# A hand-ordered attention and maxout kernel: another list of all work, three more query groups turned by DMA, six output tiles scaled on ScalarE

## The chip, the core and the metric

The program runs on one core of a Trainium2 chip. The core has a matrix engine (TensorE, PE in the profile), VectorE (DVE), ScalarE (ACT), GpSimd (POOL) and SyncE (SP), which here only issues DMA transfers. Matmuls write to PSUM, eight banks of 128 rows x 512 fp32; everything else lies in SBUF. The metric is the time of one execution on the device in microseconds, as the median of several runs.

## The reference

Four batches of 12544 queries, keys and values of 128 channels meet 49 agents per batch: the agents attend to the keys and values, the queries attend to the agents, and the result goes through a maxout layer of three 128 x 768 weights and an output weight.

```python
def sm(a, b):                      # softmax over the last axis
    s = scale * (a @ b.transpose(0, 2, 1))
    s = s - s.max(-1, keepdims=True)
    e = np.exp(s)
    return e / (e.sum(-1, keepdims=True) + 1e-09)
agent_v = sm(agents, k) @ v        # 49 x 128 for each batch
x = (sm(q, agents) @ agent_v).reshape(50176, 128)
h = np.maximum(np.maximum(x @ w1, x @ w2), x @ w3)
out = h @ w_out
```

All inputs and the output are float32; the kernel computes in bf16 with fp32 sums.

## The kernel before, in words

**Maxout by differences.** The kernel never forms `x`. For each batch it multiplies the normalised `agent_v` with three prepared matrices, w3-w1, w2-w1 and w1 @ w_out, into one tile `G` (49 agents, twice, in rows 0 to 48 and 64 to 112). With max(a, b, c) = a + max(0, c-a, b-a) a query's output is a linear part plus `wo` times max(relu(e G31), e G21), where `e` is the exponential of the query's 49 scores. The division by the sum of `e` comes last, when the output tile is scaled.

**Groups.** The 50176 queries are 49 groups of 8 tiles of 128 rows. For group `s` the steps are: load (`ql`), cast to bf16 on GpSimd (`qc`), turn so that channels are rows, scores (`sc`), exponential on ScalarE (`ex`), sums of `e` (`su`) and their reciprocals on VectorE (`re`). The turning is done in one of two ways: by eight TensorE transposes and a VectorE copy from PSUM (`qt`, `qe`), or, for the groups listed in `TURNED`, by one transposing DMA from the SP queue (`qd`).

**Six hidden blocks per group.** Block `f` has 128 hidden units for 1024 queries. In blocks other than 4, TensorE makes `u` (difference 31) into two banks, ScalarE takes relu of it to SBUF (`a`, tile `AS`), TensorE makes `v` (difference 21) into two other banks and VectorE takes the maximum of both (`x`, tile `R`). In block 4 ScalarE applies relu in place, TensorE adds `v` on top, and ScalarE applies relu again. So a group has five 128 x 1024 operations on VectorE and seven on ScalarE. `u` and `v` use rows 0 to 48 and 64 to 112 of TensorE as two 64-row halves that run beside each other.

**Output.** The output tile of a group is two banks, o = 0 and 1, each for every second tile of 128 queries. `li` adds the linear part and `p.s.o.f` the product of block `f` with `wo`. `ROWS` has a letter per group and block: with `f` a product is four matmuls with 128 rows, with `r` it is eight matmuls with 64 rows, in pairs that write to both banks at once. After the last product VectorE multiplies each bank with the reciprocals into SBUF (`ov.s.o`, tile `OS`, nine buffers) and SP stores the tile (`st`).

**Keys and values** of a batch come in chunks of up to 9 tiles of 128 rows: loads `kl`, `vl`, casts `kc`, `vc`, for batches 1 to 3 a transposing DMA of the keys (`kt`, tile `KT`), scores `ks`, exponential `kx`, product with the values `kv`, and sums `va`, `ea`. Batch 0 is done first, with TensorE transposes; the chunks of batch b+1 are mixed among the query groups of batch b.

**What sets the order.** `graph` lists every step with its engine and needs. `ORDER` is one written-out list of all 2876 steps; each engine takes its steps in that order, and the numbers behind a slash give the buffers or PSUM banks. `Plan.waits` derives the semaphore waits from the list. The `cost` and `serve` values belong to the planner that wrote the list; the program that is built doesn't use them. All instructions are issued through one recorder, so the profile gives them one line (L379 before), and groups are told apart by tile names: `ps` is PSUM, `EQ` the query exponentials, `LD` the load buffers, `QB`, `QT`, `KB`, `KT` the cast and turned tiles, `RC` the reciprocals.

Of the kernel before, what the change touches and what calls it, by code (L numbers as in the profile page):

```python
# [195 lines left out]
def dma(kb):  # L196
    return dict(cost=(0.45, 1.0), serve=kb / 415.0)


def graph(plan, em):  # L200
    add = plan.add
# [62 lines left out]
    for b in range(1, B):  # L264
        ch = chunks(b)
        for g, (t0, n) in enumerate(ch):
# [6 lines left out]
            add(f"kt{r}", SP, em.turn_by_dma("kb", "kT", r, n), (1.3, 1.0), after=[f"kc{r}"], new=[("KT", f"kT{r}")], use=[f"kb{r}"],  # L273
# [3 lines left out]
                use=[m])  # L277
# [25 lines left out]
    for s in range(NQ):  # L303
# [4 lines left out]
        if s in TURNED:  # L308
            add(f"qd.{s}", SP, em.turn_by_dma("qb.", "qT.", s, GT), (1.3, 1.0), after=[f"qc.{s}"], new=[("QT", f"qT.{s}")], use=[f"qb.{s}"],
                serve=0.255 * GT)  # L310
# [81 lines left out]
class Emit:  # L392
# [422 lines left out]
to0.3 vl0.8/2 kl0.0/8 kc0.8/0 ke0.9/2 kv0.10 kv0.5 kt0.8/0,1 ke0.2/1 vc0.3/0 kx0.11/0 kx0.7/2 vc0.2/3 ke0.8/0 wm.6/1 ks0.9/3 to0.7
kv0.3 ks0.2/7 to0.11 kt0.6/5,6 kl0.1/4 qt.0/4 ks0.8/0 kv0.11 qe.0/2 vl0.9/12 kc0.4/1 kx0.2/3 to0.2 kv0.2 kx0.8/1 kt0.4/0,1 wm.2/4
ke0.4/2 ke0.6/0 kc0.0/0 vc0.7/2 kx0.9/3 vc0.8/3 vl0.0/11 vc0.4/1 vl0.6/10 wm.1/0 ks0.4/0 ks0.6/1 sc.0/5 vl0.1/3 to0.8 kx0.6/0
ex.0/0 lw3a/7 lw1a/9 kv0.7 kt0.0/3,4 kc0.1/1 lw1b kv0.8 kt0.1/5,6 kx0.4/2 ke0.0/1 vc0.9/2 ks0.0/3 wm.0/1 to0.4 ke0.1/0 lw2a/1
kx0.0/1 lw3b kv0.4 to0.9 to0.0 ks0.1/3 vc0.0/3 kx0.1/2 vc0.6/1 vc0.1/0 lw2b wm.4/6 kv0.9 su.0/3 to0.6 to0.1 rs0/0 ql.1/6 qc.1/0
cw1 kv0.6 rc0 d31a kv0.0 kv0.1 nr0/0 d21a d31b gpa/1 lwo/5 tw1/6 re.0/0 d32 kl1.0/2 ql.2/4 cwo ew1 gpc/0 kc1.0/2 gva u.0.1/4,5  # L820
gpb/1 gvb d21b gvc u.0.2/6,7 v.0.1/2,3 a.0.1/1 kl1.1/11 u.0.0/4,5 gpd/0 x.0.1/12 qt.1/1 qe.1/2 a.0.2/0 qc.2/2 gvd u.0.3/6,7
a.0.0/2 a.0.3/1 v.0.0/2,3 pl/4 sc.1/5 x.0.0/8 vl1.0/0 el kc1.1/0 u.0.4/6,7 ex.1/1 a.0.4 kt1.0/0 v.0.3/0,1 u.0.5/4,5 x.0.3/0
v.0.2/2,3 v.0.4 u.1.1/0,1 x.0.2/5 a.0.5/2 qt.2/4 kt1.1/2 x.0.4/1 p.0.0.3/5 qe.2/2 v.0.5/2,3 a.1.1/0 u.1.0/6,7 x.0.5/6 vc1.0/3
vl1.1/2 ql.3/3 p.0.0.1 p.0.0.4 p.0.0.2 a.1.0/1 v.1.1/0,1 sc.2/4 x.1.1/4 gl/2 p.0.0.0 kl1.2/11 vl1.2/7 vc1.1/1 ks1.0/3 gvl
v.1.0/6,7 li.0/2 x.1.0/7 ex.2/2 u.1.3/0,1 kx1.0/2 su.1/4 kv1.0 re.1/3 va1.0/0 qc.3/0 p.0.0.5 p.0.1.2 kc1.2/2 u.1.2/6,7 ql.4/6
a.1.3/0 ov.0.0/0 v.1.3/3,4 u.1.4/0,1 a.1.2/1 a.1.4 x.1.3/5 p.0.1.5 ks1.1/5 p.0.1.1 p.0.1.3 v.1.2/6,7 ea1.0/0 u.1.5/3,4 kx1.1/0
p.0.1.4 p.0.1.0 kv1.1 v.1.4 vc1.2/3 x.1.2/6 v.1.5/6,7 a.1.5/0 u.2.1/3,4 x.1.4/11 kt1.2/0 a.2.1/1 ov.0.1 va1.1 p.1.0.0/2 qt.3/5
x.1.5/9 p.1.0.4 u.2.2/0,1 a.2.2/2 u.2.0/6,7 v.2.1/3,4 qe.3/0 p.1.0.2 qc.4/1 su.2/5 p.1.0.1 p.1.0.3 p.1.0.5 kl1.3/2 kl1.5/3 x.2.1/8
v.2.0/0,1 kl1.4/5 li.1/4 a.2.0/0 u.2.3/6,7 p.1.1.4 p.1.1.3 re.2/0 a.2.3/1 sc.3/5 x.2.0/0 v.2.2/0,1 u.2.4/6,7 ov.1.0/4 v.2.3/2,3
x.2.2/10 ex.3/1 kc1.3/2 p.1.1.2 p.1.1.0 ks1.2/5 u.2.5/0,1 a.2.4 kx1.2/3 v.2.4 a.2.5/2 p.1.1.5 p.1.1.1 kv1.2 x.2.3/6 ov.1.1 va1.2  # L830
x.2.4/12 v.2.5/2,3 kc1.4/1 u.3.1/0,1 qt.4/4 x.2.5/9 a.3.1/0 u.3.0/5,6 p.2.0.2/7 p.2.0.1 qe.4/0 su.3/3 v.3.1/0,1 a.3.0/2 vl1.3/11
re.3/1 sc.4/2 v.3.0/3,4 x.3.1/2 u.3.3/5,6 p.2.0.0 p.2.0.4 ex.4/0 p.2.0.5/0 li.2 v.3.3/1,2 a.3.3/1 x.3.0/1 u.3.2/5,6 a.3.2/0 ea1.1
p.2.0.3 u.3.4/3,4 p.2.1.3 p.2.1.5 a.3.4 x.3.3/7 ql.5/12 p.2.1.1 vl1.4/9 v.3.2/1,2 ov.2.0/8 u.3.5/5,6 qc.5/2 p.2.1.4 kt1.3/0
p.2.1.2 p.2.1.0 a.3.5/2 x.3.2/5 v.3.4 x.3.4/3 ov.2.1 v.3.5/1,2 u.4.1/6,7 ql.6/2 qt.5/5 p.3.0.0/0 x.3.5/4 a.4.1/1 ks1.3/3 ql.7/0
# [204 lines left out]
```

## Time and profile before

| | us |
|---|---|
| median of 3 runs (lowest, highest) | 446.41 (445.01, 449.0) |
| the profiled execution | 445.94 |
| its span | 444.1 |
| TensorE matmuls busy | 413.0 |
| TensorE weight loads busy | 258.4 |
| VectorE busy | 393.5 |
| ScalarE busy | 391.4 |
| GpSimd busy | 170.2 |

The span runs from the first to the last instruction of the profiled execution; the 1.8 us around it are launch and end. Busy times of one engine are the union of its instructions, so overlapping ones count once, and matmul ends are modelled. A group's row gives its count, its busy time, the mean of one instruction and the idle time just before it with what ended that. In the table by stretches each engine's busy us in the stretch are followed by the number of instructions in brackets, then come the granted TensorE clock, the mean busy share of the DMA engines and GB/s. The chain of work that ended last puts 65% of the span on TensorE, 10% on DMA, 9% on VectorE, 5% each on ScalarE and GpSimd.

### The profile page before, as it was taken

The numbers are of one execution on the slowest core, as the hardware profiler recorded it, in microseconds if no ns is written. First come the engines' busy times: TensorE is split into PE (matmuls) and PEld (weight loads), VectorE is DVE, ScalarE is ACT, GpSimd is POOL, SyncE is SP. The second block draws the span as 40 slices with busy tenths as digits, with TensorE's granted clock in tenths as the row PEclk, the third lists the DMA queues.
The fourth block names the chain that finished last, engine by engine and source line by source line (L and its number), as shares of the span: only waits on it lengthen the run. The fifth ranks groups of instructions, "written<-read, shape, count | busy, mean of one in ns | idle before, by whom it ended". The sixth has DMA issues, their size and how long they took to land.

```text
span 444.1 us, 14119 instructions
## 1 busy us (share of the span) xinstructions
PE 413.0 (93%) x6128; PEld 258.4 (58%) x6128; DVE 393.5 (89%) x502; ACT 391.4 (88%) x464; POOL 170.2 (38%) x177
## 2 busy tenths in 40 slices
PE   0687999999999989999899999999999999999994
PEld 0564556666666656656566666656655555655574
DVE  2336999999999989999899999999999999999994
ACT  1269999899989889999799899999999999999992
POOL 4531557645665525461844534256221000200000
PEclk9889999999999999999999999999999999999999
DMA  8999999999999999999999999999979445556333
GB/s 308 408 412 386 266 335 291 323 348 315 341 285 359 391 259 268 373 269 355 297 304 403 268 294 315 303 249 246 278 163 301 158 73 161 127 84 180 143 130 111
DMA packets 91768, 120.75 MB, mean 272 GB/s; under 512 B 65143, under 2 KB 67899, under 8 KB 91707
## 3 DMA queue, kind: packets, MB, share of 16 engines
q1 hardware_dynamic: 91504, 119.75, 91.3%
q8 instruction: 48, 0.79, 0.7%
q10 hardware_dynamic: 203, 0.10, 0.1%
q14 instruction: 13, 0.11, 0.1%
HBM read 78.74 MB, written 25.69 MB: 235 GB/s over the span
## 4 chain that ended last, share of the span: by engine, by line
PE 65%; DMA 10%; DVE 9%; ACT 5%; POOL 5%; issue 4%; SPq 1%; POOLq 0%; DVEq 0%; ACTq 0%
PE ps L379 65%; DVE R L379 6%; ACT AS L379 4%; DMA LD<-in_q_dram 3%; DMA out_dram<-OS 2%; DVE OS L379 2%; DMA KT<-KB 2%; DMA LD<-in_v_dram 2%; DMA LD<-in_k_dram 1%; POOL QB L379 1%; POOL VB L379 1%; SPq L379 1%; POOL EA L379 1%; POOL KB L379 1%; ACT R L379 1%
## 5 line engine op out<-in xcount | busy, mean ns | idle before, releaser
L379 DVE TENSOR_TENSOR R<-ps,AS 128x1024 bf16<-128x1024 f32 x245 | 293.9, 1219 | 13.9 <-PE ps L379 9.4
L379 ACT ACTIVATE AS<-ps 128x1024 bf16<-128x1024 f32 x245 | 245.3, 1029 | 16.2 <-PE ps L379 12.4
L379 PE MATMUL ps<-EQ,G 49*128 49x512 bf16 (+1 forms) x1248 | 196.6, 370 | 3.6 <-DVE OS L379 0.5
L379 PE MATMUL ps<-wo_bf,R 128*128 128x128 bf16 (+1 forms) x2984 | 187.4, 218 | 1.0 <-issue 0.8
L379 PEld LDWEIGHTS ps<-wo_bf,R 128*128 128x128 bf16 (+1 forms) x2984 | 137.1, 96 | 57.2 <-issue 37.3
L379 PEld LDWEIGHTS ps<-EQ,G 49*128 49x128 bf16 x1248 | 55.5, 93 | 70.2 <-DVE R L379 21.3
L379 POOL CAST QB<-LD 128x1024 bf16<-128x1024 f32 x49 | 51.3, 1050 | 106.3 <-DMA LD<-in_q_dram 53.0
L379 POOL CAST KB<-LD 128x1152 bf16<-128x1152 f32 (+2 forms) x45 | 50.0, 1119 | 59.4 <-DMA LD<-in_k_dram 36.3
L379 DVE TENSOR_TENSOR OS<-ps,RC 128x512 f32<-128x512 f32 x98 | 66.5, 680 | 2.9 <-DMA out_dram<-OS 1.7
L379 ACT ACTIVATE R<-ps 128x1024 bf16<-128x1024 f32 x49 | 50.2, 1025 | 2.1 <-PE ps L379 1.8
L379 ACT ACTIVATE ps<-ps 128x1024 f32<-128x1024 f32 x49 | 50.0, 1020 | 1.8 <-PE ps L379 1.2
L379 POOL CAST VB<-LD 128x1152 bf16<-128x1152 f32 (+1 forms) x33 | 37.3, 1139 | 33.0 <-DMA LD<-in_v_dram 28.5
L379 POOL TENSOR_TENSOR EA<-EA,EK 128x441 f32<-128x441 f32 x27 | 27.7, 1024 | 13.6 <-ACT EK L379 13.2
L379 ACT ACTIVATE EQ<-ps 128x512 bf16<-128x512 f32 x49 | 29.5, 601 | 2.3 <-PE ps L379 1.9
L379 ACT ACTIVATE EK<-ps 128x441 bf16<-128x441 f32 (+2 forms) x45 | 23.8, 533 | 4.4 <-PE ps L379 4.2
L379 ACT ACTIVATE VB<-LD 128x1152 bf16<-128x1152 f32 (+1 forms) x12 | 12.3, 1051 | 17.1 <-DMA LD<-in_v_dram 14.0
L379 PE MATMUL ps<-agT,KT 128*128 128x49 bf16 x392 | 17.4, 185 | 5.7 <-DVE KT L379 3.3
L379 DVE COPY QT<-ps 128x1024 bf16<-128x1024 bf16 x27 | 18.4, 681 | 3.2 <-PE ps L379 3.1
L379 PE MATMUL ps<-QT,agT 128*64 128x512 bf16 (+1 forms) x104 | 19.9, 388 | 0.0
L379 PEld LDWEIGHTS ps<-agT,KT 128*128 128x128 bf16 x392 | 14.3, 97 | 9.0 <-DVE KT L379 4.0
L379 PE MATMUL ps<-G,EQ 49*128 49x128 bf16 x392 | 19.1, 217 | 0.0
L379 DVE COPY KT<-ps 128x1152 bf16<-128x1152 bf16 (+1 forms) x12 | 8.2, 699 | 12.0 <-PE ps L379 12.0
(58 smaller groups left out, 187.4 us busy)
## 6 DMA issues: line engine op xcount, KB each, us to landing
LD<-in_q_dram SPq DMA_DIRECT2D x48, 512.0 KB, 7.2
out_dram<-OS SPq DMA_DIRECT2D x48, 512.0 KB, 5.8
LD<-in_k_dram SPq DMA_DIRECT2D x40, 576.0 KB, 7.3
LD<-in_v_dram SPq DMA_DIRECT2D x40, 576.0 KB, 8.9
LD<-in_k_dram SPq DMA_DIRECT2D x3, 512.0 KB, 7.0
LD<-in_v_dram SPq DMA_DIRECT2D x3, 512.0 KB, 7.5
LD<-in_moe_w_dram SPq DMA_DIRECT2D x6, 192.0 KB, 13.5
KT<-KB SPq DMA_TRANSPOSE x33, 7.3
```

What stands on the lines that cost most here:

```text
L379: i = call(*args, **named)
```

## The change

1. Groups 24, 27 and 29 join `TURNED`: each loses eight TensorE transposes and one VectorE copy and gains one transposing DMA on the SP queue.
2. `ROWS` has 89 letters `r` where it had 79, in other places.
3. `SCALER` is new: of the 98 output banks, six are scaled by ScalarE instead of VectorE, bank 1 of groups 3, 14, 25, 32, 47 and 48. There it takes four activations of 128 x 128 with the reciprocal as a per-row scale from SBUF, where VectorE does one 128 x 512 multiplication.
4. `ORDER` is a new list of all steps, with other buffers.
5. The planner's latency of a DMA goes from 1.0 to 1.9 us; only the list shows it.

```diff
-TURNED = (22, 25, 28, *range(30, 49))
+TURNED = (22, 24, 25, 27, 28, 29, 30, 31, 32, 33, 34, 35, 36, 37, 38, 39, 40, 41, 42, 43, 44, 45, 46, 47, 48,)
 ROWS = """
-ffffff ffffff fffrfr ffffrf ffffff rfffrf ffffff rfffrr ffffrf ffffff ffffff ffffff rfrfrr ffffff frfffr ffffff ffffff rrffff
+ffffff frrrrf ffffrf fffrff ffffff fffrrr ffffff frffrf rfrfff rffrff ffffff ffffff rfrfrr ffffff fffffr ffffff ffffff frrfff
...
+SCALER = """
+dd dd dd ad dd dd dd dd dd dd dd dd dd dd ad dd dd dd dd dd dd dd dd dd dd ad dd dd dd dd dd dd ad dd dd dd dd dd dd dd dd dd dd
+dd dd dd dd da da
+""".split()
...
 def dma(kb):
-    return dict(cost=(0.45, 1.0), serve=kb / 415.0)
+    return dict(cost=(0.45, 1.9), serve=kb / 415.0)
...
         for o in range(2):
-            add(f"ov.{s}.{o}", DVE, em.out_scale(s, o), (0.605, 0.705), use=[both[o], f"rc.{s}", plan.tile("OS", f"os.{s}")],
+            eng = ACT if SCALER[s][o] == "a" else DVE
+            add(f"ov.{s}.{o}", eng, em.out_scale(s, o, eng), (0.66, 0.82) if eng == ACT else (0.605, 0.705), use=[both[o], f"rc.{s}", plan.tile("OS", f"os.{s}")],
...
-    def out_scale(self, s, o):
-        def fn():
-            self.nc.vector.tensor_tensor(out=self.t[f"os.{s}"][:, o::2, :], in0=self.t[f"o.{s}.{o}"].rearrange("p (j c) -> p j c", c=C),
-                                         in1=self.t[f"rc.{s}"][:, 4 * o:4 * o + 4].unsqueeze(2).to_broadcast([P, 4, C]), op=ALU.mult)
+    def out_scale(self, s, o, eng):
+        def fn():
+            src, out, rc = self.t[f"o.{s}.{o}"].rearrange("p (j c) -> p j c", c=C), self.t[f"os.{s}"], self.t[f"rc.{s}"]
+            if eng == ACT:
+                for j in range(4):
+                    self.nc.scalar.activation(out[:, 2 * j + o, :], src[:, j, :], AF.Copy, scale=rc[:, 4 * o + j:4 * o + j + 1])
+            else:
+                self.nc.vector.tensor_tensor(out=out[:, o::2, :], in0=src, in1=rc[:, 4 * o:4 * o + 4].unsqueeze(2).to_broadcast([P, 4, C]),
+                                             op=ALU.mult)
         return fn
...
 ORDER = """
-kl0.5/4 id0 id ql.0/1 agl kl0.3/8 kc0.5/0 kl0.11/12 kc0.3/1 kl0.2/2 agc kl0.10/0 ones kl0.6/3 agt/0 qc.0/0 vl0.3/9 vl0.11/8
```

What the new list moves is shown at three places. First VectorE where the products of batch 2 leave PSUM (`CAST G_146`) and group 22 and 23 are in work. Before:

```order
266 L379 TENSOR_TENSOR R_123<-ps,AS_115 128x1024
267 L379 CAST G_146<-ps 128x384 x2
268 L379 TENSOR_TENSOR R_127<-ps,AS_116 128x1024
269 L379 COPY QT_105<-ps 128x1024
270 L379 TENSOR_TENSOR R_124<-ps,AS_117 128x1024
271 L379 COPY VA_148<-ps 128x49
272 L379 TENSOR_TENSOR R_129<-ps,AS_116 128x1024
```

The same place now:

```order
262 L384 CAST G_146<-ps 128x384
263 L384 TENSOR_TENSOR R_119<-ps,AS_117 128x1024
264 L384 CAST G_146<-ps 128x384
265 L384 TENSOR_TENSOR R_120<-ps,AS_115 128x1024
266 L384 COPY VA_148<-ps 128x49
267 L384 TENSOR_TENSOR R_128<-ps,AS_117 128x1024
```

The copy of group 24's turned queries (`COPY QT_105`) is gone between two maxima; what stood around it stays. Next the SP queue around the store of group 14, which is row 143 before (`OS_138`) and row 128 now (`OS_140`). `LD` are loads, `out_dram` stores. Before:

```order
135 L379 DMA out_dram<-OS_136 128x1024
136 L379 DMA LD_89<-in_k_dram 128x1152
137 L379 DMA LD_86<-in_k_dram 128x1152
138 L379 DMA LD_84<-in_v_dram 128x1152
139 L379 DMA LD_79<-in_q_dram 128x1024
140 L379 DMA LD_83<-in_v_dram 128x1152
141 L379 DMA LD_90<-in_q_dram 128x1024
142 L379 DMA LD_78<-in_q_dram 128x1024
143 L379 DMA out_dram<-OS_138 128x1024
144 L379 DMA_TRANSPOSE KT_102<-KB_94 128x9x128
```

Now:

```order
124 L384 DMA_TRANSPOSE KT_101<-KB_96 128x9x128
125 L384 DMA LD_88<-in_k_dram 128x1152
126 L384 DMA LD_89<-in_v_dram 128x1152
127 L384 DMA LD_84<-in_k_dram 128x1152
128 L384 DMA out_dram<-OS_140 128x1024
129 L384 DMA_TRANSPOSE KT_103<-KB_95 128x9x128
130 L384 DMA out_dram<-OS_141 128x1024
131 L384 DMA LD_85<-in_k_dram 128x1024
132 L384 DMA_TRANSPOSE KT_102<-KB_94 128x9x128
```

Group 14's store stood behind seven loads in a row and now stands behind three. The buffer that it empties is next written by group 19's scaling before and by group 17's now; counted in entries of the list, the store lies 25 ahead of that before and 52 now. Last, ScalarE's end, from the relus of group 48's hidden blocks on (`ps<-ps` is the first relu of its block 4, `R` the second). Before:

```order
460 L379 ACTIVATE AS_117<-ps 128x1024
461 L379 ACTIVATE AS_116<-ps 128x1024
462 L379 ACTIVATE ps<-ps 128x1024
463 L379 ACTIVATE R_127<-ps 128x1024
464 L806 UNCONDITIONAL_BRANCH
```

Now:

```order
465 L384 ACTIVATE AS_117<-ps 128x1024
466 L384 ACTIVATE ps<-ps 128x1024
467 L384 ACTIVATE OS_143<-ps,RC_131 128x128 x4
468 L384 ACTIVATE R_128<-ps 128x1024
469 L384 ACTIVATE OS_135<-ps,RC_132 128x128 x4
470 L816 UNCONDITIONAL_BRANCH
```

Four activations of group 47's output tile now stand between the two relus of group 48's block 4, and four of group 48's own tile behind them.

More of the change, by code (lines that the diff above doesn't have):

```diff
@@ L272, in graph @@
             add(f"vc{r}", POOL, em.cast("v", "vb", b, t0, n, POOL, 0, n), c, after=[f"vl{r}"], new=[("VB", f"vb{r}")], use=[f"v{r}"])
-            add(f"kt{r}", SP, em.turn_by_dma("kb", "kT", r, n), (1.3, 1.0), after=[f"kc{r}"], new=[("KT", f"kT{r}")], use=[f"kb{r}"],
+            add(f"kt{r}", SP, em.turn_by_dma("kb", "kT", r, n), (1.3, 1.9), after=[f"kc{r}"], new=[("KT", f"kT{r}")], use=[f"kb{r}"],
                 serve=0.255 * n)
@@ L308, in graph @@
         if s in TURNED:
-            add(f"qd.{s}", SP, em.turn_by_dma("qb.", "qT.", s, GT), (1.3, 1.0), after=[f"qc.{s}"], new=[("QT", f"qT.{s}")], use=[f"qb.{s}"],
+            add(f"qd.{s}", SP, em.turn_by_dma("qb.", "qT.", s, GT), (1.3, 1.9), after=[f"qc.{s}"], new=[("QT", f"qT.{s}")], use=[f"qb.{s}"],
                 serve=0.255 * GT)
@@ L815 @@
[L815 to L822, printed above, removed]
@@ L1007 @@
-x.48.4/9 p.48.1.3 p.48.0.2 st.42 p.48.1.2 ov.47.0 p.48.1.5 p.48.1.4 p.48.0.3 p.48.0.5 p.48.0.4 st.47 ov.48.1/8 ov.48.0 st.48
+kl0.5/0 kl0.6/11 agl kl0.0/10 id0 kc0.5/1 kl0.10/1 ql.0/6 ones agc id kl0.11/0 agt/0 kc0.6/0 prep kc0.0/2 kl0.8/9 kl0.4/3 qc.0/2
+vl0.11/4 kt0.5/5,6 kt0.0/3,4 kt0.6/1,2 vl0.0/5 vc0.0/3 kc0.10/2 vl0.4/7 wm.3/0 kc0.8/1 qt.0/0 wm.0/7 wm.5/7 kc0.4/0 ke0.0/1
+ke0.6/2 ke0.5/0 qe.0/0 kl0.3/9 ks0.0/7 vc0.4/2 kt0.8/1,2 kt0.10/3,4 sc.0/0 vl0.10/1 ke0.10/1 vl0.3/11 kl0.1/6 ks0.10/3 vd0.11/1
```

385 lines of the change are left out of this document (196 added, 189 removed).

## The prediction

> **What bounds the kernel now.** I read the page's busy shares first, then the busy time in stretches of 40 us.
>
> ```profile
> PE 413.0 (93%) x6128; PEld 258.4 (58%) x6128; DVE 393.5 (89%) x502; ACT 391.4 (88%) x464; POOL 170.2 (38%) x177
> ...
> core 0: us, PE busy (x) PEld busy (x) DVE busy (x) ACT busy (x) POOL busy (x), PEclk, DMA share, GB/s
> 60.00:100.00 40.00, 39.96 (x587) 25.07 (x584) 38.64 (x48) 36.93 (x45) 23.94 (x23) 1.00 1.10 323
> 100.00:140.00 40.00, 39.89 (x583) 25.04 (x581) 38.01 (x52) 37.13 (x45) 22.54 (x25) 1.00 1.10 331
> 140.00:180.00 40.00, 38.62 (x574) 24.41 (x572) 37.42 (x49) 36.34 (x44) 20.44 (x21) 1.00 1.08 297
> 180.00:220.00 40.00, 38.55 (x546) 23.62 (x541) 36.72 (x47) 36.42 (x45) 20.54 (x20) 1.00 1.04 337
> 220.00:260.00 40.00, 39.87 (x623) 25.21 (x623) 38.90 (x49) 37.62 (x47) 18.14 (x21) 1.00 1.09 315
> 260.00:300.00 40.00, 39.49 (x569) 23.91 (x566) 37.93 (x48) 38.23 (x45) 17.55 (x17) 1.00 1.14 287
> 300.00:340.00 40.00, 39.44 (x571) 23.67 (x570) 37.88 (x49) 38.48 (x48) 14.89 (x18) 1.00 0.99 245
> ...
> sum 360.00, PE 354.97 PEld 217.72 DVE 343.10 ACT 338.89 POOL 145.34; mean PE 39.44 PEld 24.19 DVE 38.12 ACT 37.65 POOL 16.15
> ```
>
> From 60 to 420 us three engines are nearly full at once: in the sum row TensorE's matmuls cover 354.97 of 360, VectorE 343.10, ScalarE 338.89. No single engine can be relieved for its full worth. Two stretches stand out: from 140 to 220 us TensorE is idle 1.38 + 1.45 = 2.83 us, while the stretches around them (100:140, 220:260) lose 0.11 and 0.13. The table of waits and the chain say what happened there:
>
> ```profile
> PEld ps L379 <- DVE R L379: 22.8, 87, 0.5
> PEld ps L379 <- ACT AS L379: 16.0, 58, 0.8
> ...
> DVE OS L379 <- DMA out_dram<-OS: 1.7, 1, 1.7
> ...
> PE ps L379 <- DMA KT<-KB: 1.2, 1, 1.2
> ...
> 154.01 7.46 DMA KT<-KB
> ...
> 205.39 10.45 DMA out_dram<-OS
> ...
> 215.93 0.69 DVE OS L379
> ```
>
> TensorE stood 1.2 us for one transposed key tile, issued at 154.01, and VectorE 1.7 us for one store, issued at 205.39 and landed 10.45 us later. The waits of the full engines on one another are many and short: TensorE's 87 on VectorE's `R` sum to 22.8 us and none is over 0.5.
>
> **The change, part by part.** The sum is made against the profiled execution, 445.94 us (span 444.1). That is 0.47 below the median of 446.41 and inside its runs (445.01 to 449.0), so I don't shift it. The prices come from the groups by shape:
>
> ```profile
> L379 DVE TENSOR_TENSOR R<-ps,AS 128x1024 bf16<-128x1024 f32 x245 | 293.9, 1219 | 13.9 <-PE ps L379 9.4 <-ACT AS L379 0.3
> L379 PE MATMUL ps<-wo_bf,R 128*128 128x128 bf16 x1720 | 134.6, 220 | 0.0
> L379 PEld LDWEIGHTS ps<-wo_bf,R 128*128 128x128 bf16 x1720 | 97.5, 97 | 42.8 <-issue 35.2 <-DVE OS L379 4.4 <-DVE RC L379 0.7
> L379 DVE TENSOR_TENSOR OS<-ps,RC 128x512 f32<-128x512 f32 x98 | 66.5, 680 | 2.9 <-DMA out_dram<-OS 1.7 <-PE ps L379 0.6
> L379 PE MATMUL ps<-wo_bf,R 64*128 64x128 bf16 x1264 | 53.4, 216 | 1.0 <-issue 0.8 <-ACT EQ L379 0.2
> L379 DVE COPY QT<-ps 128x1024 bf16<-128x1024 bf16 x27 | 18.4, 681 | 3.2 <-PE ps L379 3.1
> L379 PE MATMUL ps<-ident,QB 128*128 128x128 bf16 x216 | 16.6, 219 | 0.5 <-POOL QB L379 0.5
> L379 ACT ACTIVATE G<-ps 128x128 bf16<-128x128 f32 x4 | 1.2, 295 | 0.2 <-PE ps L379 0.2
> ```
>
> *New places of transfers, -2.0 us.* The two DMA stalls above cost 2.83 - 0.24 = 2.6 us. In the new list the store of group 14 stands behind three loads, not seven, and the closest reuse of an output buffer after its store is 24 list entries away, not 8; the closest use of a transposed key tile is 19 away, not 8. So I count most of the 2.6 as gone. Bounds: -2.8, and +2.8 if as many new stalls appear elsewhere.
>
> *Groups 24, 27, 29 turned by DMA, -1.5 us.* VectorE loses 3 copies of 0.681 = 2.04 us; TensorE loses 3 x 8 transposes at 16.6 / 216 = 0.077, 1.85 us. Both run in stretches where both engines are over 94% busy, so nearly all of it is on the path. Three transposes join the SP queue; the loads queued behind them are covered as long as the DMA is ahead (second rival). Bounds 0 and -2.04.
>
> *Four output tiles in mid-run (groups 3, 14, 25, 32), 0.* VectorE saves 0.68 each. ScalarE gains four activations of 128x128; the nearest row, the `G` evacuation of that size, gives 4 x 0.295 = 1.18. Their scale operand comes from SBUF per row, which no activation of this trace has. Groups 3 and 14 end in 60:100 and 140:180, where ScalarE is idle 3.07 and 3.66 us and VectorE 1.36 and 2.58: a gain. Groups 25 and 32 end in 260:300 and 300:340, where ScalarE is idle 1.77 and 1.52 and VectorE 2.07 and 2.12: a loss. Queued behind each tile on ScalarE is the next relu, and behind that the matmul that needs its bank. Bounds 4 x -0.68 = -2.7 and 4 x 1.18 = +4.7. The Trainium skill (ScalarE: Activation LUTs, What ACT_TABLE_LOAD costs) prices an activation with immediate scale at 186 + 0.833 N ns, adds 93 ns for a per-row pointer operand and lets neighbours overlap by 93. For 128 columns without the pointer that is 293 ns, and the trace's 295 agrees; with it, an estimate from that page is 4 x 386 - 3 x 93 = 1265 ns a tile, 0.09 above my 1.18, by which the four would cost 0.3 us more. The same page's rules advise VectorE for multiplications, which speaks against this part of the change.
>
> *Two output tiles at the end (groups 47, 48), +0.5 us.* The last us of the timeline:
>
> ```profile
> 435.95 0.40 PE L379 MATMUL ps<-wo_bf,R 64*128 64x128 bf16 x8
> 436.15 1.23 DVE L379 TENSOR_TENSOR R<-ps,AS 128x1024 bf16<-128x1024 f32 x1 [0.94 <-PE ps L379]
> ...
> 436.61 1.02 ACT L379 ACTIVATE R<-ps 128x1024 bf16<-128x1024 f32 x1 [1.54 <-PE ps L379]
> 437.29 0.68 DVE L379 TENSOR_TENSOR OS<-ps,RC 128x512 f32<-128x512 f32 x1
> ...
> 438.12 1.36 DVE L379 TENSOR_TENSOR OS<-ps,RC 128x512 f32<-128x512 f32 x2 [0.15 <-PE ps L379]
> ```
>
> Now ScalarE waits for group 47's last matmuls (436.35), scales for 1.18 until 437.5 and only then does the last relu of group 48, which started at 436.61: 0.9 us late. Behind it stand the last matmuls and both scalings. These run side by side, but ScalarE's takes 1.18 where VectorE's two took 1.36, so 0.2 returns: +0.7. Since that matmul may come earlier in the new list, I take +0.5; bounds -0.7 (one VectorE tile) and +0.9.
>
> *Ten more blocks in 64-row form, 0.* A pair block takes 53.4 / 79 = 0.68 us of matmul, a full one 134.6 / 215 = 0.63. What a full block costs besides is the weight load's 35.2 us of issue wait. Counted over TensorE's list, though, the passes between 64-row and 128-row work were 380 and are 379. The Trainium skill (TensorEngine Tiling (Array Packing), Tiling Modes) says that changing the mode drains TensorE; that fits the issue wait, and by it only the passes count, which gives 0 here as well. Bounds: ten times 35.2 / 215 = 0.16 us, -1.6, and 10 x 0.05 = +0.5.
>
> *Start, 0.* Both lists load the first batch's 24 key and value chunks and the weights before the second batch, and the first hidden blocks keep their order. The DMA, not the list, sets this stretch. Bounds +-1.
>
> Sum: 445.94 - 2.0 - 1.5 + 0 + 0.5 = 442.9, say **443 us**.
>
> **The rivals.** *VectorE alone sets the pace.* Then nine operations less count in full, 3 x 0.681 + 6 x 0.68 = 6.1 us, and the stalls' 2.6: 445.94 - 8.7 = 437.2. For it: VectorE is fuller than ScalarE in most stretches, and TensorE's weight loads fill only 217.72 of 360 us. The Trainium skill (Perfetto Trace Analysis, Identifying the Most-Contended Engine) calls matmul busy time a bad measure and weight-load busy time a good one; by it TensorE, at 60%, isn't the bound and VectorE, at 95%, is. Against it: the waits of VectorE's longest group end with TensorE (9.4 of 13.9 us).
>
> *The DMA becomes the bound: slower.* Its rows:
>
> ```profile
> q1 hardware_dynamic: 91504, 119.75, 91.3%
> ...
> KT<-KB SPq DMA_TRANSPOSE x33, 7.3
> ...
> QT<-QB SPq DMA_TRANSPOSE x22, 4.7
> ...
> 10.00:40.00 30.00, 21.67 (x327) 16.83 (x328) 11.34 (x18) 17.34 (x26) 10.76 (x11) 0.89 1.03 406
> ```
>
> The transposes move about 15.4 MB by their tiles' shapes, so plain transfers are 119.75 - 15.4 = 104.4 MB. At the 406 GB/s of 10:40 they take 257 us, 265 with its share of 1.03; q1's share is 0.913 x 444.1 = 405 us, which leaves 140 / 55 = 2.55 us of all engines for a transpose. Three add 7.7 us to a stretch whose share is over 1 from 60 to 300. If loads can't run ahead enough there, the path gets it: 445.94 + 7.7 = 453.6. The point from which it decides is TensorE waiting for key or query tiles in every group. Against it: those waits are 1.2 us now, and the DMA share falls to 0.99 after 300, so stores can move there.
>
> *ScalarE's tiles cost in full*: the first two terms as forecast, then +4.7 and +0.9: 445.94 - 3.5 + 5.6 = 448.0. For it: ScalarE is only 4 us emptier than VectorE over 360. *The list gains nothing*: other stalls for the old ones, 446.
>
> **How the numbers follow.** Forecast 0.39, its own range 440 to 446; VectorE 0.20; DMA 0.14; ScalarE 0.10; no gain 0.17. One per cent of 446.41 is 4.46, about what a measurement here tells from no change: under 441.95 is faster, over 450.87 slower. Of the forecast 0.17 lies under 441.95; with VectorE's 0.20 faster is 0.37. Slower is DMA's 0.14 and 0.03 of ScalarE's, 0.17. The rest, 0.46, is within 1%. For 8 in 10 the range runs from 436 (leaves out about 0.06, VectorE's case with more) to 451 (leaves out DMA's 0.14).
>
> **What would show it.** In the new profile: TensorE over 39.7 of 40 us in the stretches between 140 and 220, and VectorE's wait for a store gone (first term); 24 query copies and 25 query transposes with TensorE's waits on them still near 1 us (second); 24 activations of 128x128 with ScalarE no fuller than VectorE (third); the end of the last scaling over 1.85 us after the last relu's end or not (fourth); the weight load's issue wait near 35 us (fifth). The prediction is wrong if the stretches between 60 and 300 lose more than 0.5 us each, which the list alone can do in a way that no row of before shows.

## The result, and the profile after

The changed kernel takes **444.24 us** (median of 16 runs, 443.07 to 446.67), the kernel before 447.65 us (16 runs, 445.01 to 451.67). The ratio is 0.9929 with a 95% interval from 0.9902 to 0.9956: 0.7% faster, which is within one per cent. The forecast was 443 us, range 436 to 451, with "within 1%" the likeliest of the three outcomes. Three executions of the kernel before in the later calls were in a slower state and are left out of its medians.

The two profiled executions differ less than the medians: 445.94 us before and 445.17 after (spans 444.1 and 443.3). The one of before lies in the lower half of its runs, the one of after in the upper. (The section on the change says bank 1 for all six tiles of ScalarE. It is bank 0 in groups 3, 14, 25 and 32, and bank 1 in groups 47 and 48; nothing hangs on it.)

Busy time of the changed kernel in stretches of 40 us (the columns are those of the same view in the prediction):

```profile
60.00:100.00 40.00, 39.64 (x615) 25.28 (x612) 37.74 (x48) 37.87 (x47) 20.23 (x20) 1.00 1.06 319
100.00:140.00 40.00, 39.81 (x607) 25.42 (x605) 38.57 (x51) 37.57 (x46) 25.35 (x27) 1.00 1.06 330
140.00:180.00 40.00, 39.26 (x565) 24.50 (x567) 38.12 (x50) 37.92 (x50) 20.77 (x21) 1.00 1.03 286
180.00:220.00 40.00, 39.91 (x562) 25.35 (x560) 38.72 (x50) 37.70 (x46) 18.27 (x18) 1.00 1.13 331
220.00:260.00 40.00, 39.14 (x628) 24.27 (x627) 37.98 (x48) 37.42 (x46) 20.42 (x23) 1.00 1.08 330
260.00:300.00 40.00, 39.33 (x577) 23.82 (x575) 36.70 (x46) 39.03 (x50) 18.79 (x18) 1.00 1.15 276
300.00:340.00 40.00, 39.66 (x562) 23.83 (x560) 37.33 (x47) 39.23 (x52) 12.62 (x15) 1.00 1.04 295
...
sum 360.00, PE 356.21 PEld 219.82 DVE 342.90 ACT 344.88 POOL 144.60; mean PE 39.58 PEld 24.42 DVE 38.10 ACT 38.32 POOL 16.07
```

TensorE's idle time from 140 to 220 us fell from 2.83 to 0.74 + 0.09 = 0.83 us. Over the 360 us ScalarE has 6 us more work (344.88 against 338.89) and VectorE the same as before (342.90).

The gain is small in the two profiles because it is gained in one place and lost in another. The next two fences are ScalarE's rows in the timeline where the hidden blocks of group 1 and of group 48 begin (the first relu of each), before and after:

```profile
49.50 1.97 ACT L379 ACTIVATE AS<-ps 128x1024 bf16<-128x1024 f32 x2
...
428.46 1.03 ACT L379 ACTIVATE AS<-ps 128x1024 bf16<-128x1024 f32 x1
```

```profile
52.70 1.02 ACT L384 ACTIVATE AS<-ps 128x1024 bf16<-128x1024 f32 x1 [0.29 <-PE ps L384]
...
428.42 1.03 ACT L384 ACTIVATE AS<-ps 128x1024 bf16<-128x1024 f32 x1
```

Group 1 begins 3.20 us later than before. From there to group 48 the changed kernel needs 375.72 us where the old one needed 378.96: 3.24 less. From group 48's first relu to the end of the span it is 443.3 - 428.42 = 14.88 against 15.64: 0.76 less. Together +3.20 - 3.24 - 0.76 = -0.80, which is the difference of the spans.

The loss at the start shows in the column of the granted clock (the third from the right). Before and after, from 35 us:

```profile
35.00:40.00 5.00, 3.63 (x75) 2.29 (x72) 2.25 (x4) 4.96 (x7) 0.00 (x0) 1.00 1.04 379
40.00:45.00 5.00, 3.94 (x41) 1.74 (x38) 4.17 (x11) 4.36 (x6) 2.22 (x2) 1.00 1.07 382
45.00:50.00 5.00, 4.42 (x40) 1.81 (x36) 4.98 (x6) 4.80 (x7) 3.82 (x4) 1.00 0.90 233
```

```profile
35.00:40.00 5.00, 1.95 (x36) 1.39 (x32) 1.14 (x4) 3.72 (x4) 0.00 (x0) 0.72 1.04 389
40.00:45.00 5.00, 4.70 (x36) 1.86 (x32) 3.74 (x10) 3.57 (x6) 1.29 (x2) 0.50 1.07 380
45.00:50.00 5.00, 5.00 (x30) 2.04 (x30) 3.38 (x5) 3.57 (x6) 3.91 (x4) 0.50 0.93 271
```

TensorE's row in the timeline of the changed kernel after its longest pause there:

```profile
37.68 0.55 PE L384 MATMUL ps<-EK,ones_bf 128*128 128x441 bf16 x1 [2.42 <-ACT EK L384]
```

TensorE works only 1.95 of 5 us between 35 and 40, with one pause of 2.42 us, and from 40 to 50 us its clock is halved. It is "busy" 5.00 of 5 there with 30 matmuls; before, 4.42 us held 40. The Trainium skill (TensorE: Matmul & The Clock Gate, Part 1: The HAM clock gate) says that an idle window of about 3.4 us takes the clock to half speed. This trace differs: its longest pause there is 2.42 us, and the clock fell.

The groups by shape, for the parts that the change touches:

```profile
L384 DVE TENSOR_TENSOR OS<-ps,RC 128x512 f32<-128x512 f32 x92 | 62.4, 680 | 2.1 <-PE ps L384 1.7
L384 DVE COPY QT<-ps 128x1024 bf16<-128x1024 bf16 x24 | 16.4, 682 | 1.0 <-PE ps L384 1.0
L384 ACT ACTIVATE OS<-ps,RC 128x128 f32<-128x128 f32 x24 | 6.8, 373 | 0.5 <-PE ps L384 0.5
L384 PEld LDWEIGHTS ps<-wo_bf,R 128*128 128x128 bf16 x1640 | 92.9, 97 | 38.6 <-issue 31.5 <-DVE OS L384 2.8 <-DVE VA L384 0.9
```

There are 24 query copies instead of 27, so 25 groups are turned by DMA. An activation of a ScalarE tile takes 373 ns, and the 24 of them keep ScalarE 6.8 us, 6.8 / 6 = 1.13 us a tile, since neighbours overlap (four times 373 would be 1.49). VectorE no longer waits for a store: the idle time of its scalings, 2.1 us, is now put down to TensorE.

### The profile page after: what moved, and what is told of

It is laid out like the page before. It is cut to its first block, busy times and chain, and to the rows that moved or that the text cites. A ratio compares the mean times of both kernels' runs of the same rounds, so it can differ in the third digit from the quotient of the medians.

```text
span 443.3 us, 14225 instructions
## 1 busy us (share of the span) xinstructions
PE 415.9 (94%) x6184; PEld 259.7 (59%) x6184; DVE 389.2 (88%) x493; ACT 396.9 (90%) x488; POOL 169.9 (38%) x177
## 4 chain that ended last, share of the span: by engine, by line
PE 71%; ACT 14%; DMA 5%; DVE 4%; issue 3%; POOL 1%; SPq 0%; POOLq 0%; ACTq 0%; DVEq 0%
PE ps L384 71%; ACT AS L384 8%; DVE R L384 4%; DMA LD<-in_k_dram 3%; DMA LD<-in_v_dram 2%; ACT R L384 2%; ACT ps L384 1%; ACT OS L384 1%; ACT EQ L384 1%; POOL KB L384 1%; ACT EK L384 1%; SPq L384 0%; DVE avT L384 0%; DVE OS L384 0%; ACT VB L384 0%
## 5 line engine op out<-in xcount | busy, mean ns | idle before, releaser
L384 PE MATMUL ps<-EQ,G 49*128 49x512 bf16 (+1 forms) x1248 | 198.9, 374 | 2.0 <-ACT R L384 0.4
L384 POOL CAST QB<-LD 128x1024 bf16<-128x1024 f32 x49 | 50.4, 1040 | 116.5 <-DMA QT<-QB 61.0
L384 DVE TENSOR_TENSOR OS<-ps,RC 128x512 f32<-128x512 f32 x92 | 62.4, 680 | 2.1 <-PE ps L384 1.7
L384 PE MATMUL ps<-EK,VB 128*128 128x49 bf16 x392 | 17.8, 189 | 1.6 <-ACT VB L384 0.8
L384 PEld LDWEIGHTS ps<-EK,VB 128*128 128x128 bf16 x392 | 14.5, 99 | 5.5 <-ACT EK L384 2.1
```

What stands on the lines that cost most here:

```text
L384: i = call(*args, **named)
```

## Experiments

Times of one call are from one chip, beside runs of the kernel before on it. The kernel before had medians of 447.62, 446.45 and 446.70 us in the three calls. Differences are between medians; where the ratios give another size, it stands beside.

### The changed kernel again, and idle matmuls at its start

The first run is the changed kernel as it is, a control for the others of its call.

> The changed kernel unaltered, as the measure for its variants on the same chip. By its earlier runs 0.993 of the kernel before (444.2 us against 447.7).

It gave 443.68 us (442.82 to 446.44), ratio 0.9912 [0.9881, 0.9943].

The second adds 15 matmuls that nothing uses, 12 behind one step and three behind another, where TensorE stands between 35 and 40 us:

```diff
-SPARE = 8
+SPARE = 23
-ks0.7/0 to0.8 kx0.7/3 vc0.9/1 to0.7 su.0/1 rs0/1
+ks0.7/0 to0.8 wm.8/5 wm.9/5 wm.10/5 wm.11/5 wm.12/5 wm.13/5 wm.14/5 wm.15/5 wm.16/5 wm.17/5 wm.18/5 wm.19/5
+kx0.7/3 vc0.9/1 to0.7 su.0/1 wm.20/6 wm.21/6 wm.22/6 rs0/1
```

> The changed kernel with 15 more idle-time matmuls (128x512 on the identity, results unused): 12 ahead of the last chunk's total, 3 behind the first sums, where TensorE stood still for 2.4 and 0.6 us. Theory 'clock': the half-speed stretch from 37.2 to 50.9 us in the changed kernel's clock records follows from that pause and costs the 3 us by which its first groups are late; then the clock stays at full speed, group 1 starts at about 49.5 us and not 52.7, and the time falls by 2 to 3 us to 441 to 442 (0.994 of the control). Rival 'loads': the loads of the first batch and the rest of the list set the start, the clock only shows in idle time; then the time stays within 0.5 us of the control.

It gave **441.85 us** (441.42 to 443.18), ratio 0.9859 [0.9816, 0.9901], the fastest of all kernels here. Its stretches from 40 to 50 us:

```profile
40.00:45.00 5.00, 4.18 (x36) 1.77 (x37) 4.81 (x10) 4.37 (x7) 1.87 (x2) 1.00 1.07 375
45.00:50.00 5.00, 4.13 (x45) 2.10 (x43) 4.59 (x6) 4.67 (x7) 3.56 (x4) 1.00 0.98 282
```

The clock stays at 1.00, and the mean clock of its six executions is 0.987 to 0.993, against 0.977 to 0.984 in the control's twelve. ScalarE's row at the start of group 1, first of the control, then of this run:

```profile
52.51 1.02 ACT L384 ACTIVATE AS<-ps 128x1024 bf16<-128x1024 f32 x1 [1.22 <-PE ps L384]
```

```profile
49.55 1.02 ACT L384 ACTIVATE AS<-ps 128x1024 bf16<-128x1024 f32 x1 [0.33 <-PE ps L384]
```

Only idle work was added, so the halved clock, not the late data, costs these 52.51 - 49.55 = 2.96 us. The medians differ by 1.83 us (by the ratios 2.4); the profiled executions are the shortest of the six here and one above the median of the control. So much of the new list's gain is given back in the first 50 us.

### Is it one cast?

The pause of 2.42 us is behind one cast on ScalarE. This run moves the scores and the exponential that TensorE waits for ahead of it, and adds nothing:

```diff
-qc.1/0 vc0.8/0 ks0.7/0 to0.8 kx0.7/3 vc0.9/1
+qc.1/0 ks0.7/0 kx0.7/3 vc0.8/0 to0.8 vc0.9/1
```

> The changed kernel with one chunk's scores and exponential (key chunk 7 of the first batch) put ahead of ScalarE's cast of value chunk 8 instead of behind it; no extra matmuls. If the half-clock stretch of 13.65 us comes from TensorE's pause of 2.4 us behind that cast, the stretch goes or shrinks and the kernel is 2 to 3 us faster than the changed one: 441 to 442 us, clock over 0.987. If other pauses there (TensorE is busy less than 4 of 5 us from 25 to 35 us) bring it down anyway, 444 us and a clock of 0.98.

444.12 us (442.3 to 447.85), ratio 0.9938 [0.9904, 0.9972], clocks 0.973 to 0.988: no gain against the changed kernel. In its trace the clock is still halved:

```profile
35.00:40.00 5.00, 2.88 (x54) 1.73 (x52) 2.01 (x5) 4.42 (x5) 0.00 (x0) 1.00 1.04 388
40.00:45.00 5.00, 4.66 (x31) 1.74 (x31) 3.74 (x10) 3.63 (x5) 1.46 (x2) 0.51 1.08 379
45.00:50.00 5.00, 5.00 (x30) 2.02 (x30) 3.38 (x5) 3.58 (x6) 3.76 (x4) 0.50 0.94 289
```

TensorE now works 2.88 of 5 us, no pause between 30 and 40 us is longer than 0.70 us, and it still loses the clock. So the single cast isn't the cause. All 14 traces of this case fit another: TensorE was busy 1.73 to 2.88 us between 35 and 40 us in the seven in which the clock from 40 to 45 us is at 0.50 or 0.51, and 3.08 to 5.00 us in the seven in which it is at 1.00. (The first seven are the changed list without idle matmuls, the others the old list or the changed one with them.) Too little work there goes with the halved clock, and 15 idle matmuls are enough to fill it; what exactly the clock counts was not tried.

### Does the clock explain the spread of the kernel before?

In the first call, the runs of the kernel before with a mean clock of 0.989 or more took 445.15 to 447.74 us, those with less 446.42 to 451.63 us. This run adds ten idle matmuls, in the same manner. They were meant for the first 30 us; in the trace they run between 36 and 40 us:

```diff
-SPARE = 8
+SPARE = 18
-wm.4/6 kv0.9 su.0/3 to0.6 to0.1 rs0/0
+wm.4/6 kv0.9 wm.8/5 wm.9/5 wm.10/5 wm.11/5 su.0/3 to0.6 to0.1 wm.12/6 wm.13/6 wm.14/6 wm.15/6 wm.16/6 rs0/0
-kv0.0 kv0.1 nr0/0
+kv0.0 kv0.1 wm.17/7 nr0/0
```

> The kernel before with ten extra idle-filling matmuls in the places of its first 30 us where TensorE stands, nothing else. The theory that the granted clock at the start makes the two groups of times of the kernel before (clock over 0.989: 445 to 447.7, clock under 0.987: 447.5 to 451.6) says: every run over 0.989, median 446.4 or less (ratio 0.996 to 0.997) and a narrower spread than the unchanged kernel before. If the clock only marks those runs and something else makes them slow, the spread and the median stay (ratio 1.000).

447.37 us (444.95 to 450.19), ratio 1.0017 [0.9982, 1.0052]; clocks still from 0.979 to 0.993. The spread stayed, as the rival of that expectation said. It is a weak test of the clock, though: between 35 and 45 us the clock of the kernel before was at 1.00 already, and the earlier drop, 0.50 from 20 to 25 us in the trace of the kernel before, is still there at 0.66. The profiled run, one of the short ones (445.47 us), had these waits, the first between 100 and 140 us, the second between 180 and 220:

```profile
PE ps L384 <- DMA KT<-KB: 1.1, 1, 1.1
...
DVE OS L384 <- DMA out_dram<-OS: 2.2, 1, 2.2
```

Waits like the two that cost the kernel before its time from 140 to 220 us are there again, the first for another key tile (issued at 94.52 us, not 154.01): the same list meets them at other places in other executions. Whether that makes the spread stays open.

### Stores and a key transpose placed earlier in the old list

The first term alone: in the kernel before, three stores and one key transpose get earlier places.

```diff
-x.13.3/4 u.13.2/4,5 kl3.0/7
+x.13.3/4 u.13.2/4,5 kt2.3/0 kl3.0/7
-ea2.4 v.17.4 kl2.8/2
+ea2.4 v.17.4 st.9 st.14 kl2.8/2
-kv3.2 ex.26/0 ql.33/10
+kv3.2 ex.26/0 st.22 ql.33/10
...
```

> The kernel before with the stores of groups 9, 14 and 22 put ahead of the loads that they stood behind, and one transposed key load (chunk 3 of batch 2) ahead of a load; nothing else. Forecast's first term: the 1.7 us and 1.2 us stalls go, 1.5 to 2.5 us faster than the kernel before (0.995). Rival 'the list gains nothing there' (other waits come up at once): within 0.5 us of the kernel before.

446.8 us (443.1 to 448.41), ratio 0.9967 [0.9934, 0.9999]: 0.8 us less, by the ratio 1.5. The interval, 0 to 3 us, holds the forecast and reaches into the rival's. In its profile TensorE, VectorE and ScalarE no longer wait for a store, and for a key transpose only once, 0.2 us, and the two stretches are nearly whole:

```profile
140.00:180.00 40.00, 39.81 (x593) 25.11 (x591) 38.68 (x51) 37.28 (x46) 21.21 (x21) 1.00 1.08 298
180.00:220.00 40.00, 39.46 (x559) 24.67 (x556) 37.84 (x48) 36.57 (x44) 19.84 (x21) 1.00 1.03 332
```

TensorE's idle time there is 0.73 us instead of 2.83, so 2.1 us in this execution, the shortest of the twelve (443.1 us), of which the medians show 0.8.

### Groups 24, 27 and 29

In the changed kernel, their turn by TensorE and VectorE is put back:

```diff
-TURNED = (22, 24, 25, 27, 28, 29, 30, ...)
+TURNED = (22, 25, 28, 30, ...)
-v.13.5/5,6 kc2.5/2 qd.24/1 u.14.1/1,2 qt.15/7 x.13.4/5 x.13.5/1 p.13.0.2/0
+v.13.5/5,6 kc2.5/2 u.14.1/1,2 qt.15/7 x.13.4/5 x.13.5/1 qt.24/5 p.13.0.2/0
...
```

> The changed kernel with the queries of groups 24, 27 and 29 turned by TensorE and copied by VectorE again; everything else as changed. Against the changed kernel's ratio of 0.991 to the kernel before: my forecast of this term says 1.5 us slower (ratio 0.9945). The theory that VectorE alone sets the pace says 3 x 0.68 = 2.0 us slower (0.9957). The theory that the DMA is the bound says faster, by up to 7.7 us (0.974). If a transpose is wholly hidden either way, no change (0.991).

448.51 us (447.6 to 450.62), ratio 1.0045 [1.0018, 1.0072]. Against a kernel of the same call that equals the changed one in time (443.61, below) it is 4.9 us slower, three times the forecast price and more than VectorE's whole 2.04. In the trace, 260 to 300 us loses most:

```profile
260.00:300.00 40.00, 38.01 (x547) 22.94 (x547) 35.44 (x45) 37.45 (x49) 18.83 (x18) 1.00 1.01 246
```

The changed kernel has 39.33 for TensorE there. VectorE is emptier than in the changed kernel (35.44 against 36.70), though it has more to do, so its load is not what holds this stretch. That the engines wait on each other around the added steps is likely, but not shown. The places of these steps were mine, in a list that was not written for them. So the opposite was run, the kernel before with only these three groups turned by DMA:

```diff
-x.23.1/9 ks3.0/6 qt.24/0 p.22.0.2 qe.24/1 u.23.3/3,4
+x.23.1/9 ks3.0/6 p.22.0.2 qd.24/1 u.23.3/3,4
...
```

> The kernel before with groups 24, 27 and 29 turned by DMA, each near where its turn by TensorE stood (group 29's 33 entries earlier), nothing else. My forecast of this term: 1.5 us faster than the kernel before. The theory that VectorE alone sets the pace: 2.0 us faster. The theory that the DMA is the bound: up to 7.7 us slower. If the 5 us that their return to TensorE cost in the changed kernel came from places that nobody had planned for them, then 0 to 2 us faster here; if the turns themselves are worth that much, 5 us faster.

**458.98 us** (457.81 to 461.49), ratio 1.0272 [1.0226, 1.0319]: 12.3 us slower. Its two worst stretches:

```profile
180.00:220.00 40.00, 37.01 (x519) 22.95 (x519) 35.08 (x45) 35.31 (x42) 19.63 (x20) 0.99 1.05 317
260.00:300.00 40.00, 32.86 (x368) 18.85 (x365) 26.79 (x34) 27.68 (x34) 11.79 (x11) 0.83 1.00 268
```

Its waits between 200 and 300 us:

```profile
DVE OS L384 <- DMA out_dram<-OS: 8.2, 2, 4.8
...
PE ps L384 <- DVE OS L384: 7.6, 2, 4.7
...
PE ps L384 <- DMA QT<-QB: 1.5, 1, 1.5
```

And the DMA queue of SP in the timeline (start, time that the issue took, what was issued):

```profile
262.32 1.64 SPq L384 DMA_TRANSPOSE QT<-QB  x1
...
265.10 1.48 SPq L384 DMA_DIRECT2D out_dram<-OS  x3
...
278.31 3.87 SPq L384 DMA_TRANSPOSE QT<-QB  x1
```

VectorE waits 8.2 us for output buffers whose stores are late, TensorE 7.6 us behind it for the banks, and with TensorE idle for 7 of 40 us the clock falls too (0.83). In SP's queue the stores stand behind the transposes, of which the two shown take 1.64 and 3.87 us to issue; three stores go out together at 265.10. My places for the transposes are a likely cause, not a tested one: they stand 12, 9 and 36 entries ahead of the scores that use them, and 571, 91 and 79 in the changed list. Two things in the trace go beside it. From 200 to 300 us the queue itself stood 26.5 us until TensorE had done something (20.4 in the kernel before), and one of the two late stores was issued at 206.56 and landed 11.63 us later, much as the one in the kernel before that took 10.45. So this run shows what late stores and a full SP queue cost, not what the DMA can carry. The changed kernel has 25 query transposes as well and none of these waits. Neither run gives the price of the turns alone, because each also spoils a list; that stays open.

### The output tiles on ScalarE

Groups 3, 14, 25 and 32 back on VectorE in the changed kernel (the words of `SCALER` for groups 0 to 4 are shown, and so for the other three):

```diff
-dd dd dd ad dd
+dd dd dd dd dd
...
```

> The changed kernel with the output banks of groups 3, 14, 25 and 32 scaled by VectorE again, at the same places of the list. Forecast's sum (0 for these four): within 0.7 us of the control. 'VectorE alone sets the pace': 2.7 us slower. 'ScalarE's tiles cost in full': up to 4.7 us faster.

444.95 us (444.17 to 445.81), ratio 0.9926 [0.9902, 0.9951], 1.3 us more than the control of its call; by the two ratios it is 0.6, and their intervals overlap, so the times alone don't show the gain. Its stretches with groups 14 and 32:

```profile
140.00:180.00 40.00, 38.64 (x564) 24.32 (x563) 38.38 (x50) 36.66 (x44) 21.84 (x22) 1.00 1.10 319
300.00:340.00 40.00, 39.13 (x560) 23.47 (x558) 37.52 (x48) 38.21 (x48) 12.71 (x15) 1.00 1.06 303
```

TensorE has 0.62 and 0.53 us less there than in the changed kernel, about VectorE's 0.68 for a tile; the control's trace has 39.35 and 39.66, so this is not the spread of executions. So the traces show these tiles as a gain, also after 260 us, where the forecast saw a loss. The same four tiles in the kernel before, its order kept:

```diff
-dd dd dd dd dd
+dd dd dd ad dd
...
```

> The kernel before with one output tile each of groups 3, 14, 25 and 32 scaled by ScalarE, its order of work kept. Forecast: no change (bounds 2.7 faster, 4.7 slower). If the 1.3 us that these tiles gained in the changed kernel belongs to the tiles, 1.3 us faster. If it belongs to an order in which ScalarE was given room for them, as the four extra tiles suggest that cost 3.4 us in an order without that room, about 3.4 us slower.

448.62 us (446.57 to 453.16), ratio 1.0049 [1.0014, 1.0084]: 1.9 us slower. And four more tiles, of groups 8, 10, 17 and 19, in the kernel with the idle matmuls (groups 5 to 10 are shown):

```diff
-dd dd dd dd dd dd
+dd dd dd da dd da
...
```

> The changed kernel with the extra matmuls at the start (which gave 441.85 us, ratio 0.986), and four more output tiles, the second ones of groups 8, 10, 17 and 19, scaled by ScalarE. If each tile is worth what the four of the change were (1.3 / 4 = 0.33 us, because ScalarE has more room there than VectorE) it is 1.3 us faster: 440.5 (0.983). If VectorE sets the pace, 2.7 us faster (0.980). If ScalarE has no room left, up to 4 x 1.14 = 4.6 us slower (0.996).

445.29 us (443.94 to 447.75), ratio 0.9967 [0.9934, 1.0], 3.4 us more than without them (441.85, in another call; by the two ratios 4.8). What TensorE waits for tells the three lists apart. Its waits for ScalarE's tiles in the changed kernel, where no matmul waits for one and only weight loads do:

```profile
PEld ps L384 <- ACT OS L384: 0.5, 2, 0.3
```

In the kernel before with four tiles (its longest execution, 453.16 us), then in the run with four more (447.57 us, its second longest):

```profile
PE ps L384 <- ACT OS L384: 2.5, 3, 1.1
```

```profile
PE ps L384 <- ACT OS L384: 2.7, 4, 1.2
```

So a tile gains 0.2 to 0.3 us in the list that was written for it. Where it was put into the old list, or into other groups by hand, TensorE waits for it, and it costs 0.5 to 1.2. Not all of that need be the tiles: both traces also have waits of TensorE for key tiles (2.1 and 1.5 us), and the first one of VectorE for a store (3.1 us).

The tiles of groups 47 and 48 back on VectorE:

```diff
-dd dd dd dd da da
+dd dd dd dd dd dd
```

> The changed kernel with the second output tiles of groups 47 and 48 on VectorE again, as before. The prediction gave these two tiles a loss of 0.5 us, so without them 0.5 us faster (ratio 0.990). If, as the changed kernel's trace suggests, TensorE no longer waits in the last 4 us, the two tiles are a gain and without them it is 0.5 to 0.9 us slower (0.992 to 0.993); the last store then starts after two VectorE scalings of 0.68 one behind the other.

443.61 us (443.03 to 444.31), ratio 0.9929 [0.9903, 0.9955]: the ratio of the changed kernel. The last us of this run, VectorE and ScalarE:

```profile
433.58 1.23 DVE L384 TENSOR_TENSOR R<-ps,AS 128x1024 bf16<-128x1024 f32 x1
...
434.04 1.02 ACT L384 ACTIVATE R<-ps 128x1024 bf16<-128x1024 f32 x1 [0.58 <-PE ps L384]
...
435.71 1.29 DVE L384 TENSOR_TENSOR OS<-ps,RC 128x512 f32<-128x512 f32 x2 [0.30 <-PE ps L384]
```

And of the changed kernel, VectorE and ScalarE:

```profile
435.15 1.23 DVE L384 TENSOR_TENSOR R<-ps,AS 128x1024 bf16<-128x1024 f32 x1
...
435.95 1.05 ACT L384 ACTIVATE R<-ps 128x1024 bf16<-128x1024 f32 x1
...
437.49 1.14 ACT L384 ACTIVATE OS<-ps,RC 128x128 f32<-128x128 f32 x4 [0.49 <-PE ps L384]
437.93 0.69 DVE L384 TENSOR_TENSOR OS<-ps,RC 128x512 f32<-128x512 f32 x1 [1.55 <-PE ps L384]
```

From the start of the last maximum to the end of the last scaling it is 3.42 us here and 3.48 in the changed kernel. ScalarE's last relu starts 0.46 us after the last maximum here and 0.80 in the changed kernel, so the tile ahead of it delays it by 0.34 us, not by the 0.9 of the forecast. The two tiles make no difference that these runs can tell.

### Full form for 36 of the 89 pair blocks

In the changed kernel, 36 letters `r` of `ROWS` become `f`, with the list kept; group 1's, for instance:

```diff
-frrrrf
+frffrf
...
```

> The changed kernel with 36 of its 89 pair blocks in the full 128-row form again, same list; the changes between 64-row and 128-row work on TensorE's list rise by 104. If a block's form costs as little as I forecast for ten of them, the bounds for 36 are 36 x 0.05 = 1.8 us faster and 36 x 0.16 = 5.8 us slower, the forecast itself no change against the changed kernel's 444. If each change between the forms has its own price, 5.8 us slower means 0.056 us a change.

451.96 us (451.03 to 453.36), ratio 1.0117 [1.0079, 1.0156], 7.8 us more than the run of the same call that had the changed kernel's time (444.12, the moved cast). That is 7.8 / 36 = 0.22 us a block, above the upper bound of 0.16. The wait of its weight loads for issue:

```profile
PEld ps L382 <- issue: 56.0, 217, 0.5
```

The same wait in the changed kernel:

```profile
PEld ps L384 <- issue: 45.2, 178, 0.4
```

Groups by shape in this run:

```profile
L382 PE MATMUL ps<-wo_bf,R 128*128 128x128 bf16 x1928 | 154.4, 220 | 0.1
L382 DVE TENSOR_TENSOR R<-ps,AS 128x1024 bf16<-128x1024 f32 x245 | 295.0, 1219 | 21.2 <-PE ps L382 15.9 <-ACT AS L382 1.3
```

The wait grows from 45.2 us in 178 pieces to 56.0 in 217: 10.8 us in 39 more pieces, about one for each block that was changed. VectorE does the same work as in the changed kernel and waits 15.9 us for TensorE instead of 11.0. From 60 to 420 us it is busy 337.58 of 360 us (342.90 in the changed kernel), TensorE 356.68. Since the changes of form on TensorE's list rise by 104 here, 0.22 us a block and 7.8 / 104 = 0.075 us a change of form are the same measurement; the run does not part them.

## Why the prediction was right

The time and its outcome came out as forecast, with errors of opposite sign in the sum.

| step | forecast, us | what the runs showed |
|---|---|---|
| New places of transfers | -2.0 | stalls of 140 to 220 gone, 2.0 us in the trace; three stores and a key transpose alone in the old list -0.8 to -1.5 |
| Groups 24, 27, 29 turned by DMA | -1.5 | not isolated: undone here +4.9, alone in the old list +12.3 |
| Four output tiles in mid-run | 0 | -0.6 to -1.3 |
| Two output tiles at the end | +0.5 | no difference |
| Ten more blocks in 64-row form | 0 | not isolated: 0 to -2.2 |
| Start | 0, bounds ±1 | +1.8 in the medians, +3.0 in the traces |

**The first four terms of the list's run** (transfers, turns, mid-run tiles, 64-row form) were forecast at -3.5 together; from group 1 to group 48 the traces give -3.24 (-3.96 with the control's trace for the changed kernel). That agreement is of the sum, and partly luck, since the terms in it are off or not isolated. The waits named in *New places of transfers* went, and TensorE's 39.91 from 180 to 220 is over 39.7, while 39.26 from 140 to 180 is not.

***Start* is the step that failed.** "The DMA, not the list, sets this stretch" is true of when the data comes, but TensorE's clock depends on what it does while it waits, and that the list sets. The profile before showed the clock (a mean of 0.89 from 10 to 40 us) and I used that row only for the DMA's rate. The missing term is +1.8 to +3.0 us.

**It was made up for**, in part, by the mid-run tiles, whose size was wrong: 1.18 us a tile on ScalarE was right (1.13), but I let the loss after 260 us cancel the gain before. The stretch's idle sums were the wrong measure: in this list no matmul waits for a tile. The third sign failed for the same reason: ScalarE is fuller than VectorE now (344.88 against 342.90 us), and the tiles are a gain all the same. The tail's +0.5 came to nothing, and the trace fits the reason given as a possibility: the last maximum starts 6.73 us after group 48's first relu (428.42 to 435.15), before 7.69, so TensorE's work comes earlier, and ScalarE's tile delays the last relu by 0.34 us. What the turns and the 64-row form add to this is open.

***Ten more blocks in 64-row form*.** The price of a form may have been undersized. At 0.22 us a block, taken from blocks undone in a list written for pairs, ten blocks are worth up to -2.2. By the rule of the Trainium skill cited in the prediction (TensorEngine Tiling (Array Packing), Tiling Modes), that changing the mode drains TensorE, changes of mode would count, and then the term stays 0: counted over the matmuls of the traces, 64-row and 128-row work change 451 times before, 451 times now and 555 times with 36 blocks undone. The issue wait of the 128-row loads did fall, from 35.2 to 31.5 us, against the sign "near 35" that the prediction set; it fits the price per block better, but one row of two lists is no proof.

**The rivals.** *VectorE alone sets the pace* is out: VectorE's two tiles at the end cost nothing when they came back, 36 blocks that don't touch VectorE cost 7.8 us, and the time was far from 437.2. So the Trainium skill's reading (Perfetto Trace Analysis, Identifying the Most-Contended Engine), by which weight-load busy time measures TensorE and matmul busy time does not, is not borne out by this kernel: weight loads are at 59%, and the run that changes only the form of TensorE's products is the one that cost 7.8 us. *The DMA becomes the bound* did not happen: in the changed kernel none of TensorE, VectorE and ScalarE waits for a key or query transpose or for a store. The run that cost 12.3 us reached such waits in a list with the transposes put in by hand, so whether the transfers alone would ever decide was not shown. *ScalarE's tiles cost in full* is out for this list. *The list gains nothing* is out.

**The stretch sign failed.** The prediction called itself wrong "if the stretches between 60 and 300 lose more than 0.5 us each": three of six do (0.74, 0.86 and 0.67), though the control's trace doesn't repeat the 0.86 from 220 to 260 us (it has 0.21), and the time came out all the same. The stretches before summed to 3.62 us of loss and these sum to 2.91; a sum would have been the better sign.

The base was off as well: the forecast was made against one execution of 445.94 us, and the median of before turned out as 447.65, which is 1.71 more. From there the forecast change of -3.0 us leads to 444.6. The measured change is -3.41, so the change was met more closely than the time.

## What to carry to other kernels

Where three engines are each about 90% busy and a fixed list holds them together, an edit has no price of its own: the same four tiles gained 0.6 to 1.3 us in a list written for them and cost 1.9 in one that was not, and three transposes cost 12.3 us where they were put in by hand. So price an edit together with its list; undone or done alone in a list that wasn't written for it, it can cost far more than it was forecast to be worth. Look at the granted clock also in the start, where TensorE mostly waits: 15 idle matmuls there were worth 1.8 us, half of what the whole change gained.

## What the runs showed of the hardware

The halved clock stays long after TensorE is busy again. In the changed kernel the stretches 40:45 and 45:50 are at 0.50, although TensorE is busy 4.70 and 5.00 of 5 us in them. The Trainium skill (TensorE: Matmul & The Clock Gate, Part 1: The HAM clock gate) says that about 3.4 us of sustained work bring full speed back; here 4.70 + 5.00 = 9.7 us of busy time did not, nor did 4.66 + 5.00 in the run with the moved cast. The measurement decides here. What brings the clock back was not tried.
